# Hybrid linear and softmax attention on one core: projections in four column tiles, denominators for four tiles at a time, and a new instruction order

## The chip, the core and the metric

The kernel runs on one core of one Trainium2 chip. The metric is the device time of one execution in microseconds (us), the median of the runs. The engines are TensorE (PE in the profile; its weight loads are PEld), VectorE (DVE), ScalarE (ACT), GpSimd (POOL) and SyncE (SP), which issues nearly all DMAs here. Each engine works through its own list of instructions in order; semaphores tie the lists together.

## The reference, cut to what matters

One sequence of S = 2048 rows, D = 512 columns, H = 32 heads of 16. Two attention branches read the same x, and a gate per row mixes them:

```python
g = sigmoid((x * gate_w).sum(-1))
# branch A, linear attention: q, k, v = x @ A_wqkv, split into heads
pq, pk = q @ w_phi[h], k @ w_phi[h]
phi_q = concat(softmax(pq), softmax(-pq))      # 32 features a head
phi_k = concat(softmax(pk), softmax(-pk))
kv, z = phi_k.T @ v, phi_k.sum(over rows)
a = (phi_q @ kv) / (phi_q @ z + 1e-6)  ;  a = a @ A_wo
# branch B, softmax attention: q, k, v = x @ B_wqkv, split into heads
b = softmax(q @ k.T / 4) @ v           ;  b = b @ B_wo
out = g * a + (1 - g) * b
```

## The kernel before

**Branch B.** The scores are cut into 32 blocks, each of 4 heads by 512 queries; a block has 64 tiles of 128 keys by 512 queries, one head each, so there are 2048 tiles. A score tile is a matmul of 32 rows (`qk_mm`, L870): up to four of them run side by side in the four row groups of the array. Of each block, `DN[b]` tiles are turned into weights on DVE ("D tiles"), the others on ACT ("E tiles"). An E tile passes through `add_exp` (L961): one exp instruction takes two tiles, 1024 columns, out of one of two pairs of PSUM banks, so the next pair of scores (`add_qk`, the step named `qk`) must be in the other pair before ACT is through. The sum of `DN` is 682, so there are (2048 - 682)/2 = 683 exps. A D tile is written by DVE (L947, or two at a time by L937) as a 16-bit pattern, shifted twice by POOL (`shifted`, L923), and each of its three forms goes through the value matmul. A value matmul (`pv_mm`, L982) is 128 rows by 32 columns of the array: four of them, one for each head of the block, run side by side in four column tiles and add up in the bank psO ("a round" of four). `add_pv` makes the rounds of E tiles, `add_pvd` those of D tiles (`term`). After a block `add_norm` copies psO to SBUF (L1076) and normalises through small DMAs; the last two blocks do it on DVE alone (L1102 to L1112).

**Branch A and the projections.** All other matmuls are fills: `fill` takes a free PSUM bank (there are three, `MISC`), issues its matmuls in chunks, and `drain` empties the bank. `proj` (L664) makes the projections with contraction 512 or 1024, each matmul over the full 128 by 128 array and 512 columns: keys and queries of B (`k_fill`, `q_fill`), features (`phi`, names P1 for keys and P0 for queries), A's values (`va_fill`), and the output projection of each of 16 row tiles (`out_mms`: four matmuls with `oAT`, branch A's result, and four with `oT`, branch B's). B's values come from `v_fill` and `v_pair`, with 128 and 256 columns. `phi` ends in two ACT exps (L1239) and a DVE sum (L1245); for keys, two `va_fill`s then follow for each pair of row tiles, drained with the reciprocal of the sums (L1259). `kv_half` and `kfinal` make `kzbd`, which holds kv (64 columns a group) and z (4 columns a group).

Branch A's query side goes in four groups of four row tiles: `phi(0, i)` for four tiles, each written to DRAM by `q_write`; `q_turn` reads them back transposed by eight DMAs (L1315); `q_rest` makes two fills for each tile, of four matmuls with 68 columns (L1329), adds the epsilon (L1338), takes the reciprocal (L1341), multiplies (L1347) and writes the result to DRAM; `o_turn` reads it transposed into `oAT` by four DMAs (L1320). Group n + 1's transposes write the buffers that group n's matmuls read.

**The end.** The last four row tiles of the output need the last block. `out_part` adds up seven of eight matmuls of tiles 14 and 15 ahead (fills named OP14 and OP15, drained at L1167); `out_last` makes tiles 12 and 13 whole and adds the eighth matmul of 14 and 15 (L1141).

**The order.** `Plan.layout` lays out every list ahead of time: it steps through planned durations and on each engine picks the ready operation with the lowest priority value, subject to free banks. PE operations are of classes (`PE_CLASS`: score matmuls 0, value matmuls 1, all others 2); it adds 0.105 us where the class changes, and `STICK` says how far it leans to staying in class 1 or 2. A score tile for DVE may ride along with a `qk` whose row groups leave room. Where PE has nothing and its recent activity is below `ACTIVE[0]`, it places matmuls with zero weights (L972). `lock` keeps DVE and POOL instructions from overlapping. The tables `DN`, `SHIFT`, and the constants ending in `_AT`, `_PACE`, `_PRIO`, `_PAD`, `_TOL` are given numbers.

Of the kernel before, what the change touches and what calls it, by code (L numbers as in the profile page):

```python
# [30 lines left out]
DN = (6, 20, 18, 20, 26, 22, 22, 20, 22, 18, 20, 18, 22, 20, 22, 22, 26, 22, 22, 28, 22, 24, 22, 26, 18, 22, 26, 18, 20, 20, 28, 20)  # L31
# [4 lines left out]
STICK = 13.196  # L36
UNITS = 564.8
W_AT = 24.588
D_FIRST = 26
# [4 lines left out]
ACTIVE = (1.3, 0.464, 0.202, 0.534)  # L44
PE_CLASS = {"qk": 0, "dq": 0, "pv": 1, "term": 1, "zero": 1}
T_PRIO = 24.777
DQ_PRIO, DQ_K = 0.569, 1.599
KG_AT, KG_PACE, QG_AT, QG_PACE = 21.949, 5.386, 233.655, 11.179
R1_AT, R1_PACE, R2_AT, R2_PACE, R3_AT, R3_PACE = 34.139, 13.567, 134.03, 16.806, 277.767, 5.95
# [5 lines left out]
RIDE_TOL = 0.244  # L55
DMA_PAD, T2_PAD = 0.818, 1.316
QK_TOL = (0.374, 0.198)
TURN_PAD = -0.09
G_DEEP = 9
K_AT, K_PACE, Q_AT, Q_PACE = 75.929, 11.329, 287.016, 9.116  # L60
POOL_ADDS = (0, 203, 69, 203, 69, 203, 69, 195, 69, 235, 69, 203, 69, 195, 69, 202, 69, 218, 69, 203, 101, 203, 68, 195, 69, 219, 65, 203, 71, 203, 69, 203)
SHIFT = (-13.58, 13.8, -12.95, 1.31, -8.83, -3.06, 3.59, -1.48, -3.29, 1.96, -3.19, 0.72, 14.4, 6.88, 13.75, 4.89, 8.7, 7.61, 0.14, -2.86, -5.22, -8.15, -0.83, -3.77, 7.8, 2.53, -1.02, -12.66, -5.29, -0.23, -14.57, -12.4)
P64, W64 = 0.19, 0.21
M_LATE = -26.949
QK_PAD = 0.02
D1_PAIR = 1.13
PAIR_WAIT = 0.05
D_AHEAD = 21.848
CONT = -56.63
# [4 lines left out]
MARGIN = 0.403  # L74
# [45 lines left out]
class Plan:  # L120
# [57 lines left out]
    def layout(self):  # L178
# [21 lines left out]
        while left:  # L200
# [30 lines left out]
            for e in ENGINES:  # L231
# [11 lines left out]
                if e == "pe" and last_pe not in (None, "zero") and busy[e] > t - 1e-6:  # L243
# [13 lines left out]
                    if ride is not None:  # L257
                        queues[e].remove(ride)
                        heapq.heapify(queues[e])
                        pick = ride[2]  # L260
                        pick.dur = RIDE
                        used_heads |= set(pick.heads)
# [80 lines left out]
                if e == "pe":  # L343
                    cls = PE_CLASS.get(op.kind, 2)
                    if cls != last_cls:
                        op.dur += max(0.0, busy[e] + 0.105 - t)
                    last_cls = cls
                    if op.kind == "pv":
                        zero_ok, spare = op.alive, None
# [127 lines left out]
def _build(ctx, nc, A_x, A_wqkv, A_w_phi, A_wo, B_wqkv, B_wo, gate_w, out):  # L477
# [49 lines left out]
    denr = sb([128, 2, 32], F32, name="denr")  # L527
# [107 lines left out]
    def fill(prio, mms, reads, banks=None, name="", chunk=1, dur=MM, after=(), cols=NQ, cont=CONT):  # L635
# [3 lines left out]
        for i in range(0, len(mms), chunk):  # L639
# [9 lines left out]
            op.full, op.fill = cols / 2400.0 * len(part), True  # L649
# [14 lines left out]
    def proj(lhs, rhs):  # L664
        return [lambda e, ap, i=i: e.matmul(ap, lhsT=lhs[i], rhs=rhs[i], start=(i == 0), stop=(i == len(lhs) - 1))  # L665
# [27 lines left out]
    def k_fill(r, c, prio, banks=None, eng="dve"):  # L693
        f, mm = fill(prio, proj([W_B[:, t, D + 128 * r:D + 128 * (r + 1)] for t in range(KT)],
                                [xT[:, t, NQ * c:NQ * (c + 1)] for t in range(KT)]), ["wbk" if r else "wbk0"] + xk(c), banks,
                     name=f"K{r}.{c}")
# [71 lines left out]
    def q_fill(m, prio, banks=None, after=()):  # L768
# [3 lines left out]
                     name=f"Q{r}.{qc}", after=after)  # L772
# [185 lines left out]
    def add_exp(j):  # L958
        n = len(slots[j])
        base = SZ[0] * (j % 2)  # L960
        op = P.add("act", 0.051 + 0.4267 * n, 0.0, lambda e: e.activation(  # L961
# [50 lines left out]
    def add_pv(js):  # L1012
# [4 lines left out]
        for b, jmts in parts.items():  # L1017
# [30 lines left out]
            op = P.add("pe", 0.25 + 0.215 * (rounds - 1), -50, fn, reads=reads,  # L1048
# [91 lines left out]
    def last_mm(tile):  # L1140
        return [lambda e, ap: e.matmul(ap, lhsT=oT[:, 3, tile // 4, 128 * (tile % 4):128 * (tile % 4) + 128],  # L1141
                                       rhs=WoB[:, 3, :], start=True, stop=True)]

    def out_tile(qc, i):
        tile = 4 * qc + i
        if tile in SPLIT:
            f, mm = fill(O_AT + O_PACE * tile, last_mm(tile), [("oT", qc, 3), "WoB"], name=f"O{tile}")
# [5 lines left out]
        f, mm = fill(O_AT + O_PACE * (4 * qc + i), mms, reads, name=f"O{tile}")  # L1153
# [8 lines left out]
    def out_part(n):  # L1162
        tile = SPLIT[n]
        mms, reads = out_mms(tile, range(3), True)
        f, mm = fill(OP_AT + OP_PACE * n, mms, reads, name=f"OP{tile}")
# [5 lines left out]
    def out_last(i):  # L1171
        tile = 12 + i
        mms, reads = out_mms(tile, range(KT), True)
        if i < 2:
            f, mm = fill(-45, mms[:7], reads[:-2] + reads[-1:], banks=MISC + bS[:lowS], name=f"O{tile}", after=last_d1 + o_mms, cont=-45)
            last = P.add("pe", 0.25, -200 + i, lambda e: mms[7](e, f.ap()), reads=[("oT", 3, 3)], after=[mm],
                         name=f"O{tile}.7")
            last.full = 0.215
# [3 lines left out]
        else:  # L1182
            f, mm = fill(-200 + i - 1.5, last_mm(tile), [("oT", 3, 3), "WoB"], banks=bS[:lowS], name=f"O{tile}")
# [3 lines left out]
    def gate():  # L1187
        keys = []
        for c in range(QC):
# [9 lines left out]
              writes=["g1"] + keys, name="g1")  # L1199
# [14 lines left out]
    def va_fill(st, prio, after):  # L1214
        m, b = st % 8, st % 2
        f, mm = fill(prio, proj([xT[:, t, 128 * st:128 * (st + 1)] for t in range(KT)],
                                [WvA[:, t, :] for t in range(KT)]), ["WvA"] + xk(st // 4), name=f"VA{st}", after=after)
# [10 lines left out]
    def phi(qk, st, prio):  # L1228
# [4 lines left out]
                     xk(st // 4) + [("Wp", qk, t) for t in range(KT)], name=f"P{qk}.{st}",  # L1233
# [15 lines left out]
        if qk == 0:  # L1249
# [6 lines left out]
            for i in (st - 1, st):  # L1256
# [41 lines left out]
    def kfinal(prio):  # L1298
        P.add("dve", 2.3, prio, lambda e: e.tensor_tensor(
            kzbd[:, :, 0:64], kv_sb[:, :, 0:64], mask64[:].unsqueeze(1).to_broadcast([128, 8, 64]), ALU.mult),  # L1300
            reads=[("kv", 0), ("kv", 1), "mask64"], writes=["kz0"], name="kz0")
# [3 lines left out]
            reads=[("kv", 0), ("kv", 1), "mask4"], writes=["kz1"], name="kz1")  # L1305
# [19 lines left out]

    def q_rest(i, prio):
        b, j = i % 2, i % 4
        for rnd in range(2):
            mms = [lambda e, ap, gg=gg, rnd=rnd: e.matmul(  # L1329
                ap[:, 68 * gg:68 * gg + 68], lhsT=qT(4 * rnd + gg)[:, 128 * j:128 * (j + 1)], rhs=kzbd[:, 4 * rnd + gg, :],  # L1330
                start=True, stop=True) for gg in range(4)]
            f, mm = fill(prio + 0.1, mms, [("phiQT", g) for g in range(8)] + ["kz0", "kz1"], name=f"N{i}.{rnd}", chunk=4, dur=0.065, cols=68,
# [168 lines left out]
```

## Time and profile before

| what | value |
|---|---|
| median of 3 runs | 697.83 us (697.81 to 697.94) |
| the profiled execution | 699.61 us, its span 697.6 us |
| granted TensorE clock, mean | 1.000 |
| busy: PE, DVE, ACT, POOL | 676.3, 606.4, 671.3, 369.8 us |
| exps of branch B (L961) | 683, the first begins at 8.66 us, the last ends at 687.58 us |
| zero matmuls on PE (L972) | 724, in 181 rounds |

Busy time counts overlapping instructions once. The profile is of one execution, so its durations are set against its own span; the 1.8 us between its time of 699.61 and the median are not in the program.

### The profile page before, as it was taken

How to read it: one execution, taken by the hardware profiler on the slowest of the kernel's cores; microseconds unless marked ns; L12 is line 12 of the kernel's file. 1: busy time of each engine (PE TensorE's matmuls, PEld its weight loads, DVE VectorE, ACT ScalarE, POOL GpSimd, SP SyncE). 2: the span in 40 equal slices, each digit the busy share in tenths (PEclk: the TensorE clock that was granted, in tenths of full speed). 3: DMA queues.
4: the chain of work that ended last, by engine and by line, in shares of the span. 5: the costliest groups of instructions: out<-in, count | busy, mean ns of one | idle time of the engine just before them, and what ended most of it. 6: DMA issues, size and time to landing. Idle time of an engine off the chain costs nothing.

```text
span 697.6 us, 17633 instructions
## 1 busy us (share of the span) xinstructions
PE 676.3 (97%) x7281; PEld 217.7 (31%) x7335; DVE 606.4 (87%) x1020; ACT 671.3 (96%) x754; POOL 369.8 (53%) x407
## 2 busy tenths in 40 slices
PE   9999999999999999999999999999999999999999
PEld 4332233323323223333322322332223322232323
DVE  4689679998988798999987999999999998988882
ACT  6999999999999999999999999999999999999995
POOL 7165246474556552453555674657657555455542
PEclk9999999999999999999999999999999999999999
DMA  6700001001000100100003012223311123314221
GB/s 130 173 12 17 20 18 24 10 11 24 9 18 11 25 10 5 22 10 11 19 11 97 26 27 80 52 49 58 86 51 38 50 46 87 86 48 115 64 58 50
DMA packets 67455, 30.74 MB, mean 44 GB/s; under 512 B 52696, under 2 KB 62296, under 8 KB 67376
## 3 DMA queue, kind: packets, MB, share of 16 engines
q1 hardware_dynamic: 66368, 28.95, 17.7%
q8 instruction: 57, 0.93, 0.6%
q10 hardware_dynamic: 576, 0.52, 0.2%
q0 software_dynamic: 432, 0.15, 0.1%
q14 instruction: 22, 0.18, 0.1%
HBM read 7.87 MB, written 8.88 MB: 24 GB/s over the span
## 4 chain that ended last, share of the span: by engine, by line
PE 63%; DVE 18%; ACT 16%; issue 2%; DMA 1%; SPq 0%; DVEq 0%
PE psO L982 23%; PE psS L870 22%; ACT E_t L961 15%; PE psS L665 11%; PE psO L972 4%; DVE Tx_t L947 3%; DVE Ty_t L947 3%; DVE Wp_t L947 2%; DVE vA_t L947 1%; DVE oT_t L947 1%; ACT phiK_t L1239 1%; DVE stat_t L1245 1%; DVE Tz_t L947 1%; PE psS L735 1%; DMA ld<-Tf_t 1%
## 5 line engine op out<-in xcount | busy, mean ns | idle before, releaser
L961 ACT ACTIVATE E_t<-psS 128x1024 bf16<-128x1024 f32 x683 | 641.6, 1059 | 12.2 <-PE psS L870 5.8
L870 PE MATMUL psS<-qz_t,kTB_t 32*128 32x512 bf16 x2048 | 279.8, 385 | 13.8 <-ACT E_t L961 5.0
L947 DVE TENSOR_SCALAR Tx_t<-psS 128x512 int16<-128x512 f32 x218 | 144.3, 682 | 15.8 <-PE psS L870 15.0
L870 PEld LDWEIGHTS psS<-qz_t,kTB_t 32*128 32x128 bf16 x2048 | 73.4, 91 | 248.4 <-ACT E_t L961 194.1
L982 PE MATMUL psO<-E_t,vaug_t 128*32 128x512 bf16 (+1 forms) x1366 | 112.8, 385 | 0.3 <-issue 0.3
L923 POOL INT64_ADD vA_t<-vA_t x67 | 66.2, 993 | 33.8 <-PE psO L982 23.9
L947 DVE TENSOR_SCALAR Ty_t<-psS 128x512 int16<-128x512 f32 x112 | 74.0, 680 | 7.3 <-PE psS L870 7.0
L923 POOL INT64_ADD Ty_t<-Tx_t x27 | 27.2, 1006 | 64.1 <-DVE Tx_t L947 55.5
L972 PE MATMUL psO<-xT_t,zero_t 128*32 128x512 bf16 x648 | 57.4, 386 | 0.8 <-DVE Tf_t L1076 0.5
L923 POOL INT64_ADD Ty_t<-Ty_t x38 | 38.2, 1004 | 15.8 <-PE psO L982 12.7
L982 PE MATMUL psO<-vA_t,vaug_t 128*32 128x512 bf16 (+1 forms) x480 | 46.1, 383 | 0.0
L947 DVE TENSOR_SCALAR WAT_t<-psS 128x512 int16<-128x512 f32 x58 | 38.2, 679 | 3.6 <-PE psS L870 3.4
L982 PE MATMUL psO<-Ty_t,vaug_t 128*32 128x512 bf16 x398 | 40.5, 384 | 0.0
L947 DVE TENSOR_SCALAR oT_t<-psS 128x512 int16<-128x512 f32 x56 | 37.3, 684 | 3.6 <-PE psS L870 3.6
L947 DVE TENSOR_SCALAR Wp_t<-psS 128x512 int16<-128x512 f32 x58 | 38.9, 682 | 1.2 <-PE psS L870 1.1
L947 DVE TENSOR_SCALAR Tz_t<-psS 128x512 int16<-128x512 f32 x54 | 36.1, 682 | 3.5 <-PE psS L870 3.3
L947 DVE TENSOR_SCALAR vA_t<-psS 128x512 int16<-128x512 f32 x56 | 36.8, 681 | 1.0 <-PE psS L870 0.6
L982 PEld LDWEIGHTS psO<-E_t,vaug_t 128*32 128x32 bf16 x1366 | 24.3, 95 | 41.9 <-issue 39.1
L665 PE MATMUL psS<-Wp_t,xT_t 128*128 128x512 bf16 x116 | 35.6, 384 | 0.9 <-issue 0.5
L665 PE MATMUL psS<-xT_t,WB_t 128*128 128x512 bf16 x96 | 29.7, 385 | 0.8 <-issue 0.6
L923 POOL INT64_ADD vA_t<-Tx_t x20 | 18.2, 910 | 20.6 <-DVE Tx_t L947 17.3
L923 POOL INT64_ADD WoB_t<-oT_t x17 | 16.8, 987 | 21.6 <-DVE oT_t L947 21.3
(160 smaller groups left out, 870.8 us busy)
## 6 DMA issues: line engine op xcount, KB each, us to landing
dpq<-EA_t SPq DMA_DIRECT2D x16, 256.0 KB, 2.1
Rb_t<-lr SPq DMA_DIRECT2D x120, 32.0 KB, 1.8
dpo<-kv_t SPq DMA_DIRECT2D x16, 128.0 KB, 1.8
qz_t<-qz_t SPq DMA_DIRECT2D x120, 16.0 KB, 1.8
Tf_t<-Tf_t SPq DMA_DIRECT2D x60, 32.0 KB, 2.0
WB_t<-in_B_wqkv_dram SPq DMA_DIRECT2D x3, 384.0 KB, 4.4
out_dram<-WvA_t SPq DMA_DIRECT2D x8, 128.0 KB, 1.9
out_dram<-WB_t SPq DMA_DIRECT2D x6, 128.0 KB, 1.8
```

The lines of the kernel that those rows point to most:

```text
L665: return [lambda e, ap, i=i: e.matmul(ap, lhsT=lhs[i], rhs=rhs[i], start=(i == 0), stop=(i == len(lhs) - 1)) for i in range(len(lhs))]
L735: mms = [lambda e, ap, i=i, t=t: e.matmul(ap[:, 256 * i:256 * (i + 1)], lhsT=xT[:, t, NQ * c + 128 * (2 * hf + i):NQ * c + 128 * (2 * hf + ...
L870: return e.matmul(bank, lhsT=kT_B[32 * i:32 * i + 32, ROW[b // 2] % 2, 128 * kt:128 * (kt + 1)], rhs=qz[32 * i:32 * i + 32, b // 2 % 4, b ...
L923: op = P.add("pool", P64 + W64 * size, d_prio(g["ts"][0]) - 5.0 + (0.0 if key == "s" else M_LATE), lambda e: e.int64_add(words(dst), words ...
L947: ops.append(drain(f, mm, "dve", 0.70, d_prio(d), lambda e, ap, q=q: e.tensor_scalar(quarter(tb, q).bitcast(I16), ap, EXPB, 0.0, op0=ALU.a ...
L961: op = P.add("act", 0.051 + 0.4267 * n, 0.0, lambda e: e.activation(Ebuf[:, j // 2 % EPAIRS, 512 * SZ[0] * (j % 2):512 * SZ[0] * (j % 2) + ...
L972: ins = e.matmul((psO if bank is None else bank)[32 * i:32 * i + 32, :], lhsT=zero[:], rhs=xT[:, 0, 0:NQ], start=bank is not None, stop=ba ...
L982: return e.matmul(psO[32 * i:32 * i + w, :], lhsT=vaug[:, kt, o:o + w], rhs=rhs, start=start, stop=stop, tile_position=(0, 32 * i), skip_g ...
L1239: ins = e.activation(dst.rearrange("p (g s c) -> p s g c", s=2, c=64)[:, sgn, :, :], ap.rearrange("p (g c) -> p g c", c=64), ACTF.Exp, sca ...
L1245: P.add("dve", 1.22, prio, lambda e: e.tensor_reduce(sums, e3, AX.X, ALU.add), reads=[dkey], writes=[skey], name=f"ss{qk}.{st}")
```

## The change

It does five things. `columns` issues each projection matmul of 512 columns as four matmuls of 128 rows by 32 columns, one for each column tile, and such fills get the kind `col`, which is in class 1 with the value matmuls; this holds for `k_fill`, `q_fill`, `phi`, `va_fill` and the output projection, not for `v_fill`, `v_pair`, the gate, `kv_half` and the fills of `q_rest`. `z_rest` makes the denominators of a group of four row tiles in one fill of 32 matmuls with 4 columns, one DVE instruction that adds the epsilon and one reciprocal; `q_rest` is left with one fill of eight matmuls with 64 columns and one DVE multiply for each tile. Both `va_fill`s of a pair wait for the sum of the pair's second tile, where only the first did. The value matmuls of the last block get priority -95 in place of -50. The constants and tables of the order are new: the sum of `DN` is 680, its last block has 16 D tiles in place of 20; some planned durations become constants; three small DVE steps (`g1`, `kz0`, `kz1`) are locked against POOL.

```diff
-DN = (6, 20, 18, ... 20, 22, 22, 26, 22, 22, 28, ... 26, 18, 20, 20, 28, 20)
+DN = (6, 20, 16, ... 20, 20, 22, 26, 22, 24, 26, ... 28, 18, 20, 20, 32, 16)
-STICK = 13.196
+STICK = 58.273
-ACTIVE = (1.3, 0.464, 0.202, 0.534)
-PE_CLASS = {"qk": 0, "dq": 0, "pv": 1, "term": 1, "zero": 1}
+ACTIVE = (1.521, 0.344, -0.12, 0.517)
+PE_CLASS = {"qk": 0, "dq": 0, "pv": 1, "term": 1, "zero": 1, "col": 1}
-KG_AT, KG_PACE, QG_AT, QG_PACE = 21.949, 5.386, 233.655, 11.179
+KG_AT, KG_PACE, QG_AT, QG_PACE = 3.979, 2.676, 204.556, 6.371
-OP_AT, OP_PACE = 603.737, 4.0
+OP_AT, OP_PACE = 651.973, 4.0
-O_AT, O_PACE = 500.39, 18.839
+O_AT, O_PACE = 387.355, 19.09
-K_AT, K_PACE, Q_AT, Q_PACE = 75.929, 11.329, 287.016, 9.116
+K_AT, K_PACE, Q_AT, Q_PACE = 75.211, 11.97, 277.612, 9.703
+VA_LAG = 2
+STEP, RIDE_LAG, EXP_OVH = 0.0, 0.053, 0.051
+Q_END, OL_PRIO = 0.651, -22.402
...
-    denr = sb([128, 2, 32], F32, name="denr")
+    denr = sb([128, 2, 128], F32, name="denr")
...
+    def columns(e, out, lhsT, rhs, start, stop):
+        for i in range(4):
+            ins = e.matmul(out[32 * i:32 * i + 32, :], lhsT=lhsT[:, 32 * i:32 * i + 32], rhs=rhs, start=start, stop=stop,
+                           tile_position=(0, 32 * i))
+        return ins
...
     def proj(lhs, rhs):
-        return [lambda e, ap, i=i: e.matmul(ap, lhsT=lhs[i], rhs=rhs[i], start=(i == 0), stop=(i == len(lhs) - 1))
+        return [lambda e, ap, i=i: columns(e, ap, lhs[i], rhs[i], i == 0, i == len(lhs) - 1)
...
-            op = P.add("pe", 0.25 + 0.215 * (rounds - 1), -50, fn, reads=reads,
+            op = P.add("pe", 0.25 + 0.215 * (rounds - 1), -50 if b < NB - 1 else -95, fn, reads=reads,
...
+        after = [P.ops[-VA_LAG]]
         for i in (st - 1, st):
-            va_fill(i, prio, [P.ops[-2]] if i == st - 1 else ())
+            va_fill(i, prio, after)
...
+    def z_rest(n, prio):
+        mms = [lambda e, ap, j=j, g=g: e.matmul(ap[:, 32 * j + 4 * g:32 * j + 4 * g + 4], lhsT=qT(g)[:, 128 * j:128 * (j + 1)],
+                                                rhs=kzbd[:, g, 64:68], start=True, stop=True) for j in range(4) for g in range(8)]
+        f, mm = fill(prio, mms, [("phiQT", g) for g in range(8)] + ["kz1"], name=f"Z{n}", chunk=8, dur=0.028, cols=60, after=n_ops[-1:])
+        n_ops.append(mm)
+        dr = denr[:, n % 2, :]
+        plus = statq[:, 4 * (n % 2):4 * (n % 2) + 4, :].rearrange("p b (g s j) -> p (b g) s j", s=2, j=4)[:, :, 0, :]
+        drain(f, mm, "dve", 0.25, -3, lambda e, ap: e.scalar_tensor_tensor(
+            dr.rearrange("p (h j) -> p h j", j=4), plus, 1e-6, ap[:, 0:128].rearrange("p (h j) -> p h j", j=4), ALU.mult, ALU.add),
+              reads=[("sq", 4 * (n % 2) + j) for j in range(4)], writes=[("dr", n % 2)], name=f"na{n}")
+        P.add("dve", 0.9, -3, lambda e: e.reciprocal(dr, dr), reads=[("dr", n % 2)], writes=[("dr", n % 2)], name=f"nb{n}")
+
     def q_rest(i, prio):
-        b, j = i % 2, i % 4
-        for rnd in range(2):
-            mms = [... four matmuls, rhs=kzbd[:, 4 * rnd + gg, :] ...]
-            drain(... na: 128x16 ...); P.add(... nb: reciprocal 128x16 ...); drain(... nd: 128x256 ...)
+        b, j, n = i % 2, i % 4, i // 4
+        mms = [lambda e, ap, g=g: e.matmul(ap[:, 64 * g:64 * g + 64], lhsT=qT(g)[:, 128 * j:128 * (j + 1)], rhs=kzbd[:, g, 0:64],
+                                           start=True, stop=True) for g in range(8)]
+        f, mm = fill(prio + 0.1, mms, [("phiQT", g) for g in range(8)] + ["kz0"], name=f"N{i}", chunk=8, dur=0.036, cols=64,
+                     after=n_ops[-1:] + (ow_ops[i - 2:i - 1] if i > 1 else []))
+        drain(f, mm, "dve", 0.69, -3, lambda e, ap: e.scalar_tensor_tensor(
+            oA[:, b, :].rearrange("p (g j d) -> p g j d", g=8, j=4), ap.rearrange("p (g j d) -> p g j d", g=8, j=4),
+            egate[:, i:i + 1], dr3, ALU.mult, ALU.mult), reads=[("dr", n % 2), "eg"], writes=[("oA", b)], name=f"nd{i}")
...
-            f, mm = fill(-45, mms[:7], reads[:-2] + reads[-1:], banks=MISC + bS[:lowS], name=f"O{tile}", after=last_d1 + o_mms, cont=-45)
+            f, mm = fill(OL_PRIO, mms[:7], reads[:-2] + reads[-1:], banks=MISC + bS[:lowS], name=f"O{tile}", after=last_d1 + OL_AFTER * o_mms, cont=-45, kind="col")
```

More of the change, by code (lines that the diff above doesn't have):

```diff
@@ L242, in layout @@
                     active = sum(w * (y - max(x, t - WINDOW)) for x, y, w in streams) / WINDOW
[L243 removed]
+                if e == "pe" and last_pe not in (None, "zero", "col") and busy[e] > t - 1e-6:
                     want = {"qk": "dq", "dq": "dq"}.get(last_pe, "term")
@@ L648, in fill @@
                        after=after if prev is None else [prev], name=f"{name}.{i}")
-            op.full, op.fill = cols / 2400.0 * len(part), True
+            op.full, op.fill, op.kind = cols / 2400.0 * len(part), True, kind
             if prev is None:
```

103 lines of the change are left out of this document (44 added, 59 removed).

## The prediction

> **What bounds the kernel now.** I read the page first, then the groups by shape, then the engines in order of time in a few windows, and last the end of the span.
>
> ```profile
> PE 676.3 (97%) x7281; PEld 217.7 (31%) x7335; DVE 606.4 (87%) x1020; ACT 671.3 (96%) x754; POOL 369.8 (53%) x407
> PE 63%; DVE 18%; ACT 16%; issue 2%; DMA 1%; SPq 0%; DVEq 0%
> ```
>
> The second line is the chain that ended last: PE holds 63% of it, though ACT is as busy. The groups say why.
>
> ```profile
> L961 ACT ACTIVATE E_t<-psS 128x1024 bf16<-128x1024 f32 x683 | 641.6, 1059 | 12.2 <-PE psS L870 5.8 <-PE psO L982 3.8
> L982 PE MATMUL psO<-E_t,vaug_t 128*32 128x512 bf16 x1355 | 112.8, 385 | 0.3 <-issue 0.3
> L665 PE MATMUL psS<-Wp_t,xT_t 128*128 128x512 bf16 x116 | 35.6, 384 | 0.9 <-issue 0.5 <-ACT phiK_t L1239 0.3
> L1347 DVE SCALAR_TENSOR_TENSOR kv_t<-psS,gT_t,denr_t 128x256 bf16<-128x256 f32 x32 | 14.8, 477 | 0.6 <-DVE denr_t L1341 0.2
> L1259 DVE RECIPROCAL stat_t<-stat_t 128x128 f32<-128x128 f32 x8 | 7.6, 946 | 0.1
> L1341 DVE RECIPROCAL denr_t<-denr_t 128x16 f32<-128x16 f32 x32 | 7.2, 239 | 0.3
> L1338 DVE SCALAR_TENSOR_TENSOR denr_t<-statq_t,psS 128x16 f32<-128x16 f32 x32 | 4.9, 162 | 0.0
> ```
>
> Exps overlap, so what counts is start to start. In order of time, half of the 683 exps start 0.904 us after the one before. All 683 at that pace would take 617.4 us, the 32 pairs of feature exps add 0.98 us each (31.4), and the stretch from the first exp (8.66) to the last one's end (687.58) is 678.9 us. So some 30 us of the exp loop are waits that the busy share hides, 10.0 us lie behind the last exp and 8.7 ahead of the first. The waits look like this, on PE and then on ACT:
>
> ```profile
> 325.84 0.40 PE L982 MATMUL psO<-Ty_t,vaug_t 128*32 128x512 bf16 x4
> 326.07 0.39 PE L982 MATMUL psO<-oT_t,vaug_t 128*32 128x512 bf16 x4
> 326.29 0.39 PE L982 MATMUL psO<-Tx_t,vaug_t 128*32 128x512 bf16 x4
> 326.50 0.39 PE L982 MATMUL psO<-Ty_t,vaug_t 128*32 128x512 bf16 x4
> 326.82 0.40 PE L870 MATMUL psS<-qz_t,kTB_t 32*128 32x512 bf16 x4
> 327.25 2.85 ACT L961 ACTIVATE E_t<-psS 128x1024 bf16<-128x1024 f32 x3 [0.30 <-PE psS L870]
> ```
>
> Four rounds of value matmuls (0.22 us from round to round) and the step to row tiles (0.32, so 0.10 more) make the scores late, and ACT idles. I went through every exp that starts over 0.02 us late (146, 28.0 us lost together) and looked at what PE had run between the last two score groups: 40 times four value or zero rounds (8.89 us), 36 times three (5.08), 27 times two or fewer (7.90), 15 times a mix of projection and value matmuls (3.36), 28 times something else (2.8). A mix:
>
> ```profile
> 294.44 0.60 PE L665 MATMUL psS<-WvA_t,xT_t 128*128 128x512 bf16 x2
> 294.98 0.62 PE L982 MATMUL psO<-E_t,vaug_t 128*32 128x512 bf16 x8
> 295.52 0.39 PE L870 MATMUL psS<-qz_t,kTB_t 32*128 32x512 bf16 x4
> ```
>
> PE also ran 181 zero rounds (181 x 0.22 = 40 us), so it is not full; it is late in places. DVE is fullest where branch A's query side runs: busy 307.0 of 341 us from 347 to 688, 289.9 of 338 before.
>
> **The change part by part.**
>
> Exps: 2048 - 680 D tiles leave 684 exps, one more: **+0.9 us**, with nothing to hide it, since ACT is never ahead. Two D tiles less save DVE 2 x 0.68 us and PE one round; I count nothing for them.
>
> Column tiles: 440 projection matmuls (the weight-load rows of L665 and L1141: 128 for features, 120 for keys and queries, 64 for A's values, 128 for the output) become 1760. A round of four value matmuls takes as long as one full matmul (both 0.215 to 0.225 us start to start), so the work stays as it is. What goes is the step between the two shapes: 50 times a projection matmul stands next to a value or zero matmul, at 0.32 in place of 0.22 us: 50 x 0.10 = 5.0 us of PE. The steps to and from score matmuls stay at 0.32. On the path lie at least the 15 late mixes above: 15 x 0.10 = **-1.5 us**; ends 0 (PE waits elsewhere) and -5.0. I take the counted one.
>
> Weight loads: a full load lasts 97 ns and a 32-column load 95 ns (both groups' means), and four of the latter hide under each value round today. A rule of the Trainium skill speaks against this part: "TensorEngine Tiling (Array Packing)", Restrictions and Gotchas, says that column tiling excludes fast weight load, so the projections would lose it. It is weighed as the last rival.
>
> Denominators, DVE: now 4.9 + 7.2 + 14.8 = 26.9 us. After: 16 multiplies of 512 columns at 0.746 (the instruction of the same kind and size at L1136) = 11.9; four reciprocals of 128 columns at 0.946 (L1259) = 3.8; four additions of 128 columns, between 162 ns (16 columns) and 477 (256), by the line between them 0.31, = 1.2. Together 16.9: 10 us saved. DVE has 18% of the chain: **-1.8 us**; ends 0 and -10. If it isn't DVE that is late, PE is next.
>
> Denominators, PE: 128 matmuls of 68 columns start 37 ns apart; with 64 columns they cost the same. New are 128 matmuls of 4 columns; the nearest row is the gate's 64 with 1 column, 25 ns apart: 128 x 25 = 3.2 us. In chunks of eight (16, plus 16 of the multiplying fills, as against 32 now) the steps between shapes stay equal. At PE's 63% of the chain **+2.0 us**; ends 0 (in place of zero matmuls) and 3.2. Each group's four multiplies now wait for one fill and its 0.946 us reciprocal; behind them on DVE stand only that group's own steps, and DVE's list is laid out around them.
>
> Both V fills of a pair behind one sum: today the second one's matmuls can run early and then hold one of three banks (in one pair from 169.94 until DVE empties it from 174.85, the sum ending at 173.40). Afterwards its four matmuls, 0.9 us, fall into the 1.45 us between the two: 0; eight pairs at one class step of 0.10 either way give ends of -0.8 and +0.8. The three locks touch three instructions of 2.5 us in all: 0.
>
> The end, on PE, DVE and ACT:
>
> ```profile
> 686.89 0.81 PE L665 MATMUL psS<-WoA_t,phiK_t 128*128 128x512 bf16 x3 [0.16 <-issue]
> 688.28 0.40 PE L982 MATMUL psO<-E_t,vaug_t 128*32 128x512 bf16 x2
> 688.83 1.04 PE L665 MATMUL psS<-WoA_t,phiK_t 128*128 128x512 bf16 x4
> 690.55 0.71 DVE L1112 STREAM_TRANSPOSE oT_t<-Rb_t 128x512 bf16<-128x512 bf16 x1
> 694.44 0.69 ACT L1179 ACTIVATE WB_t<-psS,gT_t 128x512 bf16<-128x512 f32 x1 [1.47 <-PE psS L665]
> ```
>
> Tile 14's part runs from 686.66 to 688.2, between the last exp and the last value matmuls. With these first, the normalising on DVE starts earlier, but PE works without a break until 694.2 (25 matmuls behind 688.83), and the moved ones only change places with them. A gain comes where parts 14 and 15 (14 matmuls) are done before: 7 of the 25 x 0.215 = 1.5 us. Room comes from the last block's four fewer D tiles: 12 value matmuls less, three rounds, for one round of E tiles. Half of it: **-0.8 us**; ends 0 and -1.5.
>
> The order: PE, DVE and the class steps freed above, and a fill that may now share a run with value rounds, let four- and three-round runs be split. They cost 8.89 + 5.08 = 14.0 us. If one in four goes: **-3.5 us**. The trace cannot show the new order; half of them gone is -7.0, and as much more waiting is +7.0. I take the fourth, as PE and DVE both have some 1% less to do in the same time.
>
> Sum: +0.9 - 1.5 - 1.8 + 2.0 - 0.8 - 3.5 = -4.7 us. The profiled execution (699.6, span 697.6) becomes 694.9; its 1.8 us over the median stay what they are, and 697.8 - 4.7 = **693.1 us**.
>
> **The rivals.**
>
> *The relief is swallowed.* PE's freed time becomes zero matmuls, late runs stay late, and only the exp and the end move: 697.83 + 0.9 - 0.8 = 697.9. For it: 40 us of zero rounds are there already, and 7.9 of the 28 us are lost though PE had run only two value rounds or fewer. Against: 63% of the chain is PE.
>
> *The order gives its better end.* Half of the long value runs gone (-7.0), the end at -1.5, the 5.0 us of class steps by PE's chain share (-3.2), DVE's as above (-1.8), the new matmuls in idle time: 0.9 - 7.0 - 1.5 - 3.2 - 1.8 = -12.6, so 685.2; it spans 685 to 689.
>
> *The denominators hold up the query side* (slower). All four tiles of a group wait until PE has run four chunks, each behind a score group (4 x 0.904 = 3.6 us), then 0.31 + 0.95 on DVE: with the multiply 5.9 us from the last transpose to the first result, where it is 1.2 now; say 3.5 more for each group, and group n + 1's transposes wait for group n: 14 us by the last. Its `oAT` transposes are issued until 679.6 and land 2.7 later, at 682.3; the first matmul that needs them starts at 686.66. So it decides from 4.4 us of delay on. Beyond it, 14 - 4.4 = 9.6 us go to the end, whose gain is lost as well: 693.1 + 9.6 + 0.8 = 703.5. Against: the four tiles of a group are spread over 18 to 38 us today, by waits for other work, and have half the fills afterwards.
>
> *The weight loads show.* If the four loads of 95 ns are not hidden, a projection round takes 380 ns, not 220: 440 x 0.16 = 70 us more, 768. Against: value rounds load the same way today, at 0.22 a round. By the rule of the Trainium skill cited above, the loads would be slower and the change could be such a loss; the value rounds do not bear it out.
>
> **How the numbers follow.** Chances: forecast 0.60 (690 to 696), relief swallowed 0.13, better order 0.12, query side late 0.13, weight loads 0.02. A measurement of this kernel can tell about 0.2%, 1.4 us. Faster takes the first and third and a little of the second, 0.74; the same most of the second, 0.10; slower the rest, 0.16. The range 686.5 to 700 leaves out the two slow cases (0.15) and the low part of the better order (0.05).
>
> **What would show it.** Right: 684 exps; projection groups by four at 0.22 us a round and no 0.32 step beside value rounds; 16 multiplies near 0.75 us and four reciprocals near 0.95; fewer exps late behind four value rounds; the chain's PE share below 63%; the stretch from the last exp's end to the end of the span at 9 to 10 us. Wrong: a projection round over 0.25 us; as many late exps as now (146); matmuls waiting for `phiK_t` transposes in the last 12 us; a granted clock under 1.000, which would mean that the new thresholds for zero matmuls let PE cool, for which nothing is in the sum.

## The result, and the profile after

The kernel after takes **691.46 us** (691.33 to 691.72, four runs) against 697.88 (697.81 to 698.09, four runs) before: a ratio of 0.9908, interval 0.9891 to 0.9925, so 6.4 us less. The forecast was 693.1 with a range of 686.5 to 700. The profiled execution takes 691.33, its span 689.2, and the granted clock is 1.000 in all four runs. It lies at its median, whereas the profiled execution of before lay 1.8 us above its own: the two profiles differ by 8.4 us in the span, the medians by 6.4.

Busy time and the chain that ended last, from the page of after:

```profile
PE 678.5 (98%) x8759; PEld 218.5 (32%) x8759; DVE 599.5 (87%) x927; ACT 670.3 (97%) x755; POOL 368.8 (54%) x403
PE 76%; ACT 21%; DVE 2%; issue 0%
```

The two PE numbers don't compare as they stand: before's trace has 7281 matmul rows for 7335 weight loads, and the 54 matmuls without a row are all projections. The kernel with before's lists and column tiles (below), whose trace has every row, shows PE busy for 684.7 us; after has 678.5. The chain now runs over PE and ACT almost alone; DVE has gone from 18% to 2%. The groups by shape (out<-in, count, busy time and mean, idle time ahead) that answer to those of before:

```profile
L973 ACT ACTIVATE E_t<-psS 128x1024 bf16<-128x1024 f32 x684 | 640.7, 1064 | 4.5 <-PE psS L882 1.6
L643 PE MATMUL psS<-Wp_t,xT_t 128*32 128x512 bf16 x512 | 41.4, 384 | 0.6 <-DVE Tx_t L959 0.3 <-ACT EA_t L1250 0.3
L643 PEld LDWEIGHTS psS<-Wp_t,xT_t 128*32 128x32 bf16 x512 | 10.5, 94 | 16.8 <-issue 9.7 <-DVE Ty_t L959 1.5 <-DVE Tx_t L959 1.0
L1358 DVE SCALAR_TENSOR_TENSOR kv_t<-psS,gT_t,denr_t 128x512 bf16<-128x512 f32 x16 | 11.7, 741 | 0.0
L1348 DVE RECIPROCAL denr_t<-denr_t 128x128 f32<-128x128 f32 x4 | 3.8, 945 | 0.0
L1345 DVE SCALAR_TENSOR_TENSOR denr_t<-statq_t,psS 128x128 f32<-128x128 f32 x4 | 1.1, 278 | 0.0
```

The idle time in the first line matters most: ACT was idle 4.5 us ahead of its exps, and 12.2 before. In time, the stretch from the first exp to the last one's end went from 678.9 to 670.1 us, though there is one exp more. The stretch ahead of the first exp lost 0.5, and the one behind the last exp gained 0.9: -8.8, -0.5 and +0.9 make the 8.4 of the two spans. The view of the waits on ACT (waiting line, releaser, us in all, times, the longest) says which waits went. Before:

```profile
ACT E_t L961 <- PE psS L870: 5.8, 16, 1.1
ACT E_t L961 <- PE psO L982: 3.8, 3, 1.5
```

After:

```profile
ACT E_t L973 <- PE psS L882: 1.6, 4, 1.0
ACT E_t L973 <- PE psO L994: 0.7, 2, 0.4
```

The second kind is the long one: an exp finds no free buffer in the ring of twelve until value matmuls have read one. In the timeline of before, two such waits end at 346.25 and 388.15 us, each behind the rounds of E tiles that free the buffer:

```profile
345.39 0.81 PE L982 MATMUL psO<-E_t,vaug_t 128*32 128x512 bf16 x8
346.25 1.02 ACT L961 ACTIVATE E_t<-psS 128x1024 bf16<-128x1024 f32 x1 [1.47 <-PE psO L982]
387.48 0.62 PE L982 MATMUL psO<-E_t,vaug_t 128*32 128x512 bf16 x8
388.15 1.02 ACT L961 ACTIVATE E_t<-psS 128x1024 bf16<-128x1024 f32 x1 [1.21 <-PE psO L982]
```

Five exps of before start over 1.5 us after the one ahead of them (135.94 to 137.94 us, 343.58 to 346.25, 374.43 to 376.61, 385.91 to 388.15, 447.99 to 450.15). Together that is 11.2 us where five steps of 0.904 would be 4.5: 6.7 us lost in five places. Three of them are the waits for the ring, the other two (137.94 and 376.61) wait for scores. After has no such place. Counted as in the prediction, the late exps fall from 146 (28.0 us) to 125 (18.2 us): 9.8 us less. With the 0.9 us of the one exp more, that is the 8.8 us by which the stretch got shorter, within 0.1.

What PE ran between the last two score groups ahead of each late exp can be told in both kernels from the weight loads, which have all their rows:

| PE ran | before: late exps, us | after: late exps, us |
|---|---|---|
| four or more value or zero rounds | 40, 8.9 | 34, 7.1 |
| three | 32, 4.6 | 21, 2.7 |
| two or fewer | 15, 5.5 | 11, 2.2 |
| a mix of projections and value rounds | 32, 4.9 | 25, 3.1 |
| projections alone | 11, 2.4 | 13, 1.1 |
| something else | 16, 1.8 | 21, 2.1 |

The five long places are 6.7 of the 9.8 us; they stand in the lines three, two or fewer, and projections alone.

### The profile page after: what moved, and what is told of

Same layout as the page of the kernel before. It is cut to its first block, busy times and chain, and to the rows that moved or that the text cites. A ratio compares the mean times of both kernels' runs of the same rounds, so it can differ in the third digit from the quotient of the medians.

```text
span 689.2 us, 20447 instructions
## 1 busy us (share of the span) xinstructions
PE 678.5 (98%) x8759; PEld 218.5 (32%) x8759; DVE 599.5 (87%) x927; ACT 670.3 (97%) x755; POOL 368.8 (54%) x403
## 4 chain that ended last, share of the span: by engine, by line
PE 76%; ACT 21%; DVE 2%; issue 0%
PE psO L994 27%; PE psS L882 26%; ACT E_t L973 20%; PE psS L643 14%; PE psO L984 5%; PE psS L747 1%; PE psS L1352 1%; PE psS L984 1%; PE psS L734 1%; PE psS L1339 1%; DVE Tx_t L959 1%; PE psS L595 0%; DVE Ty_t L959 0%; PE psS L1216 0%; ACT EA_t L1250 0%
## 5 line engine op out<-in xcount | busy, mean ns | idle before, releaser
L959 DVE TENSOR_SCALAR Tx_t<-psS 128x512 int16<-128x512 f32 x206 | 135.2, 679 | 11.8 <-PE psS L882 10.4
L994 PE MATMUL psO<-E_t,vaug_t 128*32 128x512 bf16 x1368 | 112.3, 384 | 0.0
L959 DVE TENSOR_SCALAR Ty_t<-psS 128x512 int16<-128x512 f32 x104 | 69.0, 682 | 10.7 <-PE psS L882 10.5
L984 PE MATMUL psO<-xT_t,zero_t 128*32 128x512 bf16 x604 | 54.3, 386 | 0.2 <-DVE Tf_t L1088 0.2
L643 PE MATMUL psS<-Wp_t,xT_t 128*32 128x512 bf16 x512 | 41.4, 384 | 0.6 <-DVE Tx_t L959 0.3
L994 PE MATMUL psO<-Ty_t,vaug_t 128*32 128x512 bf16 (+1 forms) x384 | 40.5, 383 | 0.0
L643 PE MATMUL psS<-xT_t,WB_t 128*32 128x512 bf16 x464 | 36.5, 384 | 0.7 <-ACT phiK_t L1250 0.5
L959 DVE TENSOR_SCALAR Wp_t<-psS 128x512 int16<-128x512 f32 x52 | 34.5, 679 | 2.4 <-PE psS L882 2.3
L959 DVE TENSOR_SCALAR vA_t<-psS 128x512 int16<-128x512 f32 x48 | 31.3, 677 | 1.8 <-PE psS L882 1.0
L935 POOL INT64_ADD WoB_t<-oT_t x16 | 16.2, 1013 | 30.8 <-DVE oT_t L959 30.1
L949 DVE TENSOR_SCALAR Tx_t<-psS 128x1024 int16<-128x1024 f32 x21 | 25.5, 1215 | 7.2 <-PE psS L882 6.8
```

Source lines behind the costliest of these rows:

```text
L643: ins = e.matmul(out[32 * i:32 * i + 32, :], lhsT=lhsT[:, 32 * i:32 * i + 32], rhs=rhs, start=start, stop=stop, tile_position=(0, 32 * i))
L935: op = P.add("pool", P64 + W64 * size, d_prio(g["ts"][0]) - 5.0 + (0.0 if key == "s" else M_LATE), lambda e: e.int64_add(words(dst), words ...
L949: return e.tensor_scalar(dst[:, a[0]:a[1] + 1:a[1] - a[0], :].bitcast(I16), src[:, b[0]:b[1] + 1:b[1] - b[0], :], EXPB, 0.0, op0=ALU.add, ...
L959: ops.append(drain(f, mm, "dve", 0.70, d_prio(d), lambda e, ap, q=q: e.tensor_scalar(quarter(tb, q).bitcast(I16), ap, EXPB, 0.0, op0=ALU.a ...
L984: ins = e.matmul((psO if bank is None else bank)[32 * i:32 * i + 32, :], lhsT=zero[:], rhs=xT[:, 0, 0:NQ], start=bank is not None, stop=ba ...
L994: return e.matmul(psO[32 * i:32 * i + w, :], lhsT=vaug[:, kt, o:o + w], rhs=rhs, start=start, stop=stop, tile_position=(0, 32 * i), skip_g ...
```

## The experiments

The theory to be tested: the saved steps on PE and the saved time on DVE are worth more than their shares of the chain, because the order picked for after spends them against single long waits. The rivals: the parts alone bring the gain in any order; the tables and constants alone bring it; the end brings it. "After's order" below means that every engine's list is the one of after, instruction by instruction. A half-clock window is a stretch of 3.41 us (or twice that) in which the clock records show 0.5 granted; over a whole execution one is a mean clock of 0.998.

**Full matmuls in after's order.** The lists keep their order; each projection is one matmul over the full array again.

```diff
-        for i in range(4):
-            ins = e.matmul(out[32 * i:32 * i + 32, :], lhsT=lhsT[:, 32 * i:32 * i + 32], ... tile_position=(0, 32 * i))
+        ins = e.matmul(out, lhsT=lhsT, rhs=rhs, start=start, stop=stop)
```

> The changed kernel with the same order on every engine, but each projection matmul is issued over the full array again. Theory 1 (freed PE time counts): projections now stand next to value or zero matmuls 89 times, each step costs 0.10 us, 8.9 us of PE; at PE's 63 to 76% of the chain 5.6 to 6.8 us come back, 697 to 698 us. Theory 2 (the order alone makes the gain): under 2 us come back, 691.5 to 693.5. A projection round stays at 0.22 us in both.

Measured: 696.89 us, 5.4 more than after. Of its ten runs, six have one half-clock window, some 1.3 us more each, and one has several (701.56); the three at full clock take 695.6 to 695.8, 4.3 more than after. In the profiled run (695.63, clock 1.000) the last output is issued at 690.48 us, 5.8 later than in after; it then lands in 1.7 us, where after's takes 3.95 (see the tail below), so the span is 4.4 longer. In after's order 89 projections stand beside value or zero rounds (74 in before's by the weight loads; the 50 of the prediction are those whose matmuls have rows): 89 x 0.10 = 8.9 us of steps, of which 5.8 came back, 65%. A round lasts the same either way (0.215 to 0.226 us), so this is the step between shapes and not the weight loads. The late exps say the same: 142 (24.0 us) in place of 125 (18.2), and 4.5 of the 5.8 us between the two stand behind mixes of projections and value rounds, 42 (7.6) in place of 25 (3.1).

**Column tiles alone, in before's order.** The kernel before with its own lists; only the emission of L665 and L1141 changes.

```diff
-        return [lambda e, ap, i=i: e.matmul(ap, lhsT=lhs[i], rhs=rhs[i], ...)
+        return [lambda e, ap, i=i: [e.matmul(ap[32 * c:32 * c + 32, :], lhsT=lhs[i][:, 32 * c:32 * c + 32], ...) for c in range(4)][-1]
```

> The kernel before with its own order on every engine, but each projection matmul is issued in four column tiles. The mirror of the run that put full matmuls back. Theory 1 (freed PE time counts wherever it is freed): 50 steps of 0.10 us, 1.5 us (the late mixes alone) to 3.2 us less, 694.7 to 696.4. Theory 2 (freed time is worth something only in an order made for it): 698 within 1.

Measured: 696.50 us (695.74 to 696.88), ratio 0.9974 [0.9964, 0.9984], 1.6 us less than before. That is the size of the -1.5 that the prediction counted from 15 late mixes. By the weight loads before has 32 of them (4.9 us), and this kernel 15 (2.2). Of 74 steps, 7.4 us of PE, 1.6 us came back, 22%. Four of the five long places are still there (exps at 137.23, 345.16, 385.77 and 447.67 us), whereas full matmuls in after's order leave one (175.95): they go with the lists, and not with the shape of the projections. The two runs and the two kernels together, by lists (after's hold the new denominators too):

| | full matmuls | column tiles |
|---|---|---|
| before's lists | 698.0 | 696.5 |
| after's lists | 696.9 (695.7 at full clock) | 691.5 |

**The old cost of the denominators on DVE, in after's order.** Each multiply becomes two of 256 columns, each behind a 16-column addition and reciprocal whose results nobody reads. By the durations of before's rows that is 16.2 us more on DVE, spread over the 16 tiles.

```diff
-        drain(f, mm, "dve", 0.69, -3, lambda e, ap: e.scalar_tensor_tensor(oA[:, b, :] ...
+        halves = ... 2 x (scalar_tensor_tensor 128x16, reciprocal 128x16, scalar_tensor_tensor oA[:, b, 256 * hf:256 * hf + 256])
+        drain(f, mm, "dve", 0.69, -3, halves, ...
```

> The changed kernel with the same order, but each of the 16 multiplies is split into two of 256 columns, each behind a small addition of 16 columns and a reciprocal of 16 columns whose results nobody uses: DVE gets 32 x (0.162 + 0.239) + 16 x (2 x 0.477 - 0.741) = 16.2 us more, somewhat over the 10 us that the change saves. Theory 1 with DVE at 18% of the chain as before: +2.9 us, 694.4. Theory 2, or DVE at its 2% of the chain after: +0.3, 691.8. If DVE were the bound in that stretch: +10 or more, over 701.

Measured: 697.16 us, 5.7 more than after. Neither expected number is right, and the trace shows that less was put back than meant. None of the added instructions reads what another has written, and they overlap. DVE is busy for 606.1 us, where after has 599.5:

```profile
PE 683.3 (98%) x8759; PEld 219.2 (31%) x8759; DVE 606.1 (87%) x1007; ACT 672.3 (97%) x755; POOL 368.2 (53%) x403
```

From the first instruction of such a tile to the next one behind the tile it takes 1.10 us, and after's single multiply 0.66: 16 x 0.44 = 7.0 us put back. With overlaps counted once, these steps keep DVE for 25.8 us in before, 16.6 in after and 23.6 here, so three quarters of the 9.2 us that the change saves are put back, and they cost 5.7 us, 81%. The longer steps also hold the fill's PSUM bank some 0.4 us longer; the run doesn't tell the two apart. The chain of this kernel shows DVE at only 6%:

```profile
PE 73%; ACT 19%; DVE 6%; issue 1%; DMA 1%; POOL 0%; POOLq 0%
```

**Parts and tables crossed.** Four kernels are planned anew, each with a structure and a set of tables and constants (`DN`, `STICK`, `ACTIVE`, the paces, `SHIFT` and so on): before with column tiles and its own tables, before with the new denominators and its own tables, all of after's structure with before's tables, and before's structure with after's tables.

```diff
 first:   PE_CLASS with "col": 1, columns(...) in proj and the output, tables of before
 second:  z_rest and the q_rest of after, tables of before
 third:   after.py, tables of before
 fourth:  before.py, tables of after
```

> The kernel before with the column tiles alone (the kind col and its class too), planned again with the constants of before. Theory 1 (freed PE time counts wherever it is freed): 50 steps of 0.10 us less, 5.0 us of PE at 63% of the chain, -3.2 us, 694.7. Theory 2 (the freed time is only worth something in an order made for it): 698 within 1.5.

> The kernel before with the denominators for four tiles alone, planned again with the constants of before. Theory 1: 10 us of DVE less, by the run with 16.2 us put back (5.7 us slower, 35%) -3.5 us, and 3.2 us of PE more at 63%, +2.0: 696.4. Theory 2: 698 within 1.5. Rival: the query side is held up behind one fill for four tiles, 700 or more.

> The changed kernel with its column tiles, denominators, V pairs and last sums, but with the tables and constants of before (the new constants set so that they do nothing). Theory 1: most of the gain stays, -4 to -5 us, 693 to 694. Theory 2: most of it goes, 696.5 to 699.

> The kernel before with the tables and constants of the changed one and nothing else (one more exp, 684). Theory 1: the order alone is worth nothing or is a loss, since its places are made for less PE and DVE work: 698 to 702. Rival (the order alone makes the gain): 691.5 to 694.

Measured, in order: 719.47 us (ratio 1.0301 [1.028, 1.0322]), 707.95 (1.0137 [1.0116, 1.0158]), 705.76 (1.0102 [1.0074, 1.0129]) and 731.49 (1.0469 [1.0428, 1.051]). All are slower than both kernels:

| | before's tables | after's tables |
|---|---|---|
| before's structure | 697.9 | 731.5 |
| after's structure | 705.8 | 691.5 |

Neither column tiles, nor denominators, nor tables brought anything by themselves in the order that was laid out for them. Each of these four is one order only, and the next two runs show how far orders of one structure lie apart, so the table puts no price on a part. Most of the time lost goes to the wait for the ring. One line of the waits on ACT of each, the kernel with column tiles first, then the new denominators, after's structure with before's tables, and before's structure with after's tables:

```profile
ACT E_t L967 <- PE psO L988: 20.8, 11, 3.9
```

```profile
ACT E_t L961 <- PE psO L982: 10.0, 5, 5.4
```

```profile
ACT E_t L973 <- PE psO L994: 8.8, 6, 3.7
```

```profile
ACT E_t L965 <- PE psO L986: 27.6, 12, 6.3
```

Set against 3.8 us in before and 0.7 in after, these waits are 17.0, 6.2, 5.0 and 23.8 us longer than before's, while the kernels are 21.2, 9.7, 7.5 and 33.3 us slower than before beside them. All four profiled runs have half-clock windows (mean clock 0.988 to 0.998). In three of them one wait for the ring ends inside such a window or within 1.6 us behind it (3.85 us of the first kernel's, 3.7 of the third's, 1.6 of the fourth's), so the windows are a part of these waits too; in the third kernel that is most of the difference.

**One constant moved.** After, with `MARGIN` at 0.400 in place of 0.401, and with `K_AT` one us later.

```diff
-MARGIN = 0.401
+MARGIN = 0.400
```

```diff
-K_AT, K_PACE, Q_AT, Q_PACE = 75.211, 11.97, 277.612, 9.703
+K_AT, K_PACE, Q_AT, Q_PACE = 76.211, 11.97, 277.612, 9.703
```

> The changed kernel with one planned latency (MARGIN) at 0.400 in place of 0.401 us, so that the order comes out another way from some point on; all else as it is. If the measured order is a picked one among many: 693 to 706. If every order planned with these tables does as well: 691.5 within 1.

> The changed kernel with the start of branch A's key side (K_AT) 1 us later in the plan. As the run before: a picked order 693 to 706, any order 691.5 within 1.

Measured: 699.88 us (ratio 1.0021 [1.0005, 1.0038]) and 717.84 (1.0281 [1.0261, 1.0301]), 8.4 and 26.4 more than after. Five of the ten runs of the first have half-clock windows; the other five take 698.9 to 699.5, 7.6 more than after. A step of one nanosecond in one constant of the planner is worth more than the whole change. The ring in the waits on ACT, first and second:

```profile
ACT E_t L973 <- PE psO L994: 5.9, 6, 2.6
```

```profile
ACT E_t L973 <- PE psO L994: 21.0, 9, 9.9
```

In the first, this wait is 5.2 us longer than in after, and the stretch behind the last exp is 13.2 us in place of 10.9: together 7.5 of the 7.6 us between the two spans.

**The last block's sums at their old place.**

```diff
-            op = P.add("pe", 0.25 + 0.215 * (rounds - 1), -50 if b < NB - 1 else -95, fn, reads=reads,
+            op = P.add("pe", 0.25 + 0.215 * (rounds - 1), -50, fn, reads=reads,
```

> The changed kernel, planned again with the last block's value matmuls at the old priority of -50. As predicted, PE works through the same matmuls to the end either way, so nothing changes: 691.5 us within 0.5. Rival: the last block's sums first are worth their 0.5 to 1.5 us, 692.0 to 693.0.

Measured: 691.61 us (690.44 to 692.31) against after's 691.46: no difference that these runs can tell. The traces tell more. The lists are those of after up to 665 us, and the last output is issued 6.60 us behind the last exp's end, where after has 6.39: the sums first are worth 0.2 us there. The time hides it, since this kernel's last output lands in 1.85 us, and after's in 3.95 (the next run says why); its span ends with the zero matmuls on PE instead, at 689.2 us.

**No zero matmuls behind the last real one.** After's PE list ends with 64 zero matmuls, during which the last outputs are written. They are taken off.

```diff
+    while P.order["pe"][-1].name == "idle":
+        P.order["pe"].pop()
```

> The changed kernel without the 64 zero matmuls behind the last real matmul. Theory A: the last block of instructions, 16 KB fetched from 685.80 to 687.42, holds up the packets of the last output, which lands 3.95 us after its issue in place of 1.72 before the change; with 128 instructions fewer that fetch goes or comes earlier, and 2.2 us are saved, 689.3 us. Theory B: the landing is late for another reason, nothing changes, 691.5 us.

Measured: 689.85 us, ratio 0.9885 [0.987, 0.9899], 1.6 less than after. Two of its four runs have a half-clock window (690.4 and 690.6), the two without one take 689.2, 2.2 less than after. The timeline of after's end:

```profile
679.63 1.24 PE L643 MATMUL psS<-WoA_t,phiK_t 128*32 128x512 bf16 x16
683.52 3.83 PE L984 MATMUL psS<-xT_t,zero_t 128*32 128x512 bf16 x64
683.94 0.69 ACT L1190 ACTIVATE WB_t<-psS,gT_t 128x512 bf16<-128x512 f32 x1 [0.82 <-PE psS L643]
684.65 0.35 ACTq L1134 DMA_DIRECT2D out_dram<-WB_t  x1
```

From 684.65 the last output takes until 688.60 to land. The DMA view of after from 684 us on has, beside the two queues of outputs, an instruction fetch, and its issues (KB each, median us to landing) are:

```profile
out_dram<-WB_t SPq DMA_DIRECT2D x1, 128.0 KB, 1.7
out_dram<-WB_t ACTq DMA_DIRECT2D x1, 128.0 KB, 3.9
```

The same view without the zeros:

```profile
out_dram<-WB_t ACTq DMA_DIRECT2D x2, 128.0 KB, 1.7
```

In after the last block of instructions, 16 KB, is fetched from 685.80 to 687.42 us, across the output. Without the zeros the program has one fetch less (68, not 69), and the last of that size runs from 680.99 to 682.09, ahead of every output. Up to the issue of the last output the two tails agree: 6.33 us from the last value matmul in both. Two runs above bear this out. With full matmuls in after's order the 64 zeros are still there, the last such fetch runs from 682.99 to 684.02, ahead of the outputs, and the last one lands in 1.72 us: the zeros by themselves don't hold it up. With column tiles in before's order a fetch runs from 690.65 to 691.64, across two other outputs (issued at 689.53 and 690.19), and these land in 3.24 and 2.90 us, where the same two of before take 1.85 and 1.70. Their line in that kernel's DMA view:

```profile
out_dram<-WB_t SPq DMA_DIRECT2D x2, 128.0 KB, 3.1
```

**The best of both.** The fill of 32 matmuls with four columns (`Z0`) runs at 421.6 to 423.4 us. Without the zeros, the profiled run shows half clock right behind it, from 424.4 to 427.8 us; so do the profiled runs with the last sums at their old place (423.9) and with the old cost on DVE (423.7). This kernel takes the zeros off and puts one full matmul of 384 columns, into columns that nobody reads, ahead of each chunk of eight in that fill.

```diff
+        if n == 0:
+            mms = [m if k % 8 else lambda e, ap, m=m: (e.matmul(ap[:, 128:512], lhsT=qT(0)[:, 0:128], rhs=xT[:, 0, 0:384], ...), m(e, ap))[1] ...]
+    while P.order["pe"][-1].name == "idle":
+        P.order["pe"].pop()
```

> The changed kernel without the zero matmuls at the end, and with one full matmul of 384 columns (0.16 us, its result unused) ahead of each eight small ones of the first denominators' fill. If those small matmuls let the clock fall to 0.5 for one window of 3.41 us at 420 to 428 us in some executions: that goes, 689.2 us with the clock at 1.000, against 689.85. If the clock fell for another reason: 689.9 or, by the 0.64 us added, 690.5.

Measured: 689.62 us (689.35 to 690.08), ratio 0.9877 [0.9863, 0.9892], span 687.5, clock 1.000 in all four runs. It beats both kernels, after by 1.8 us. Against the kernel without the zeros the medians don't differ by more than the runs do: it is 0.4 slower than that kernel's two runs at full clock, and 0.9 faster than the other two. The views by windows (PE, PEld, DVE, ACT and POOL busy, clock, DMA share, GB/s), first without the zeros, then this kernel:

```profile
424.00:426.00 2.00, 2.00 (x22) 0.51 (x20) 1.33 (x2) 1.44 (x2) 0.34 (x1) 0.60 0.44 159
426.00:428.00 2.00, 2.00 (x26) 0.95 (x26) 1.80 (x2) 1.81 (x2) 0.69 (x1) 0.55 0.40 134
```

```profile
424.00:426.00 2.00, 2.00 (x29) 0.69 (x28) 1.75 (x3) 1.66 (x3) 0.29 (x1) 1.00 0.48 170
426.00:428.00 2.00, 2.00 (x34) 0.78 (x31) 1.89 (x3) 1.97 (x3) 1.08 (x2) 1.00 0.34 119
```

PE counts as busy for all of both windows; the sixth number, 0.60 and 0.55 against 1.00, is the granted clock. Four runs each are few: that the full matmuls, and not chance, kept the clock up is likely and not shown. Matmuls of four columns are not the only way to such a window either: the kernel with column tiles and before's tables has three of them and no such matmul, and the one with before's structure and after's tables has one.

## Why the prediction was right, and where its steps were off

The time and its sign were right, 6.4 us less against 4.7. That the number came so close is luck in good part: after's last output lands 2.2 us late, for a reason that the prediction did not have, and without that (no zero matmuls at the end, full clock) the kernel takes 689.2 us, 8.7 less than before. Two of the signs that it named for being right failed: PE's share of the chain rose from 63% to 76%, and the stretch behind the last exp is 10.9 us, not 9 to 10. By its own steps:

- **Exps, +0.9.** Held: 684.
- **Class steps, -1.5.** The size held in before's order, where the part alone gave -1.6, but not the count under it. The 50 steps and 15 late mixes were taken from matmul rows, and 54 of the 440 projection matmuls have none in that trace; by the weight loads it is 74 steps and 32 late mixes. In the order after the term was under-sized: 89 projections stand beside value or zero rounds, and their steps are worth 5.8 us up to the last output, beyond the bound of -5.0. Mixes still make exps late, 25 times (3.1 us), but less than full matmuls do in the same order, 42 times (7.6).
- **Weight loads.** A column load takes 94 ns, four are hidden, and a round takes as long as a full matmul: the last rival is refuted. The rule of the Trainium skill cited with it ("TensorEngine Tiling (Array Packing)", Restrictions and Gotchas) may hold of the load itself; no run here shows a cost in the time.
- **Denominators on DVE, -1.8.** The saving was sized well (16.6 us left, forecast 16.9). Its worth was not: in after's order 5.7 of 7.0 us put back were lost, 81% in place of the chain's 18%; the full 9.2 us at that share would be some 7.5, an estimate. The chain's share tells where one path ran in one execution, not what DVE delays besides: before's lists with column tiles show DVE at 8% of the chain, and the run with the time put back at 6%.
- **Denominators on PE, +2.0.** The pitch held, 25 ns from start to start, so 3.2 us for the 128. What part lay on the path was not measured by itself. Missing from the sum: the half-clock window that comes behind the first of these fills in some executions.
- **V fills and locks, 0.** Nothing in the traces speaks against it. The two locked multiplies of `kzbd` take 0.68 and 0.95 us, where they took 1.45 and 0.18.
- **The end, -0.8.** The sign of PE's part held: from the last exp's end to the issue of the last output it is 6.39 us, where before has 7.57, so -1.2. The span behind the last exp grew by 0.9 all the same, since the output's landing took 3.95 us in place of 1.72; without the zeros it is 8.7 us, 1.3 less than before. The prediction followed PE, DVE and ACT to the last issue and held the landing constant. The last block's sums first, which it named as the lever, are worth 0.2 of the 1.2.
- **The order, -3.5.** The size and the mechanism held in part: late exps behind four or three value rounds went from 13.5 us to 9.8, 3.7 less, a little over one in four; 1.1 of it is the long place at 137.94 us. Left out were the other places: those behind two rounds or fewer and behind projections alone lost 4.6 us more, with the other four long ones in them. The prediction had the waits behind two rounds or fewer in hand, and used them only as evidence for "the relief is swallowed".
- **"Its 1.8 us over the median stay what they are".** They did not. One of the five long places (376.61 us, PE 1.03 us behind a DVE drain) is absent from the run with column tiles in the same order, so it likely belongs to that execution; that would be 1.3 of the 1.8, and the rest stays open.

The rivals "relief swallowed" and "query side held up" are refuted too: the late exps are fewer, and no matmul of the end waits for a transpose. More than any term, the form of the sum failed. It adds parts and an order, and they do not add: column tiles are worth 1.6 us in before's lists and 4.3 at full clock in after's, and the steps and the DVE time, each put back alone into after's lists, cost 4.3 and 5.7 us, more than the 6.4 of the whole. That the long waits went with the lists is shown by the two runs that hold the lists fixed. Which steps of the picked order remove them is open; the runs show only that the four crossed kernels and the two with a moved constant bring long waits back.

## What to carry to other kernels

Where a planner lays out the lists, cost a change with the lists held fixed, in the old order and in the new (here 1.6 and 4.3 us for column tiles), and treat each new order as a draw whose spread is measured by moving one constant by next to nothing: here +8 and +26 us. Emit full-array work in the array shape of its neighbours when it stands between them; it costs more instructions, and frees 0.10 us of PE at each joint, of which 22% reached the time in one order and 65% in the other. When time is put back to price it, read from the trace how much was put back (7.0 us here, not 16.2). Compare matmul rows with weight loads before counting neighbours. Follow the last output until it lands: instructions that come late in the program, idle ones too, can be fetched while it is being written, and the DMA view counts both as a share of the same 16 engines.

## What the runs showed of the hardware

- An instruction fetch of 16 KB across the last output made its landing 3.95 us in place of 1.72. Taking 64 idle matmuls off the end moved the fetch and gave the 2.2 us back. Another fetch, across two outputs of another kernel, made them 3.24 and 2.90 in place of 1.85 and 1.70.
- A change between full-array matmuls and column rounds costs 0.10 us on PE: 0.32 us from start to start, where two of the same shape take 0.215 to 0.226.
- The clock fell to 0.5 for one window of 3.413 us behind 32 matmuls of four columns, at the same place in three profiled runs of after's lists, in a stretch for which the trace calls PE busy throughout. The Trainium skill, "TensorE: Matmul & The Clock Gate", The HAM clock gate, describes a free-running window of 3413 ns and half rate; the trace agrees with both. Two other executions of the program without the zeros kept the full clock, as all four of after did.
- The cost of one such window is about 1.3 us here: 696.6 to 697.6 against 695.6 to 695.8 with full matmuls in after's order, 690.4 to 690.6 against 689.2 without the zeros. In before, four runs at a mean clock of 0.998 took 700.8 to 701.3 against 698.0 or so, some 3 us more.
